# Attention on whole 128-row tiles with rows of zeros, and a DRAIN of GpSimd behind the fourth output block of every group

## The chip, the cores and the metric

The kernel runs on one core of one Trainium2 chip. The metric is the device time of one execution in microseconds, the median of several runs; less is better. A profile comes from one further execution. The engines are named as the profile has them: PE is TensorE, PEld its weight loads, DVE VectorE, ACT ScalarE, POOL GpSimd and SP SyncE, which only issues DMAs here.

## The reference

Three steps follow one another: attention against mean-pooled keys and values, a top-1 mixture of experts (MoE), and a dense layer that takes the maximum of three products.

```python
# q, k, v: (8, 8, 576, 64); q and k are scaled by 8 in the set-up
k_p = k.reshape(B, H, Sp, 8, D).mean(axis=3)          # Sp = 72
v_p = v.reshape(B, H, Sp, 8, D).mean(axis=3)
scores = np.matmul(q, k_p.transpose(0, 1, 3, 2)) / np.sqrt(D)
attn = softmax(scores)                                # max subtracted, sum + 1e-9
x = np.matmul(attn, v_p)                              # -> (4608, 512)

xn, en = x / (norm(x) + 1e-6), expert_emb / (norm(expert_emb) + 1e-6)
logits = xn @ en.T / tau                              # 8 experts
for e in range(8):                                    # expert_idx = argmax(logits)
    h = np.maximum(x[mask_e] @ w1[e], 0.0)            # w1: (512, 1024)
    out[mask_e] = gate_w[mask_e, None] * (h @ w2[e])

h = np.maximum(np.maximum(out @ w1, out @ w2), out @ w3)   # 512 -> 768
return h @ w_out                                           # (4608, 512)
```

## The kernel before, in words

**Attention.** The 4608 tokens make 36 tiles of 128. Two neighbouring batches share nine tiles: four of the first batch, one mixed tile with 64 tokens of each, and four of the second. So 32 tiles belong to one batch and 4 are mixed. A batch has 576 pooled rows (8 heads of 72), which are held as five chunks of 128, 128, 128, 128 and 64 rows (`RC`). Only the fifth chunk isn't full.

The main loop (from L1481) is a software pipeline over tiles. One turn issues, in this order, the scores of tile it-1 (`stage_s`, L421: products at L442, or L428 for a mixed tile; maximum and subtraction on DVE, L457 and L460), the transposes of the attention weights of tile it-3 (`stage_a`, L468: five transposes at L473, two copies on ACT at L475 and L476), the transposes of q for tile it (`stage_q`, L406), the exponential of tile it-1 on ACT (`stage_e`, L466), and attention times v of tile it-4 (`stage_x`, L488: six products at L496, then five steps on DVE, L506 to L523). Each float32 product stands in the trace as two passes, that is two LDWEIGHTS and two MATMULs. Between the DVE steps `fill()` puts pieces of the routing, in numbers from a small table (L913).

Beside the tiles run the preparations of the next batches (`prep_steps`, L254): the keys and values are pooled (on DVE for the first batches, L263 and L271, else on GpSimd, L277 and L287), spread over head slots with a mask (`spread_v`, L293, into `vbd`), transposed (`trans_k` L305 and `trans_v` L341 for the first two batches, `trans_kv` L318 for the others), and multiplied with the normalised expert embeddings `enT` (`vdot`, L350; two DVE steps at L358). The last chunk is handled with 64 rows throughout: in the transposes, in `vdot` and in `stage_x`, where the contraction runs over `RC[c]` rows. `vT` and `enT` hold 64 partitions, so `vdot` contracts 64 rows in every chunk. The tiles `kp`, `vp`, `vT` and `aT` come from rotating pools.

**MoE.** Its items run from the gather of x in expert order through two products (L1062 and L1110) with weights split into two parts. Its first work overlaps the last attention tiles.

**Last layer.** `second` (L1572) works in six groups of 768 tokens. After its products a group has six output blocks of 128 tokens. For each block TensorE makes 18 products (`out_part`, L1697), and `out_rows` scales the sum by the gate on ACT into `ob` (L1703, five buffers) and issues an indirect DMA on GpSimd that scatters the 128 rows to the output (L1704). These DMAs write the same tensor, and each is issued after the one before has landed. GpSimd's instructions run in the order of the code. Behind the six blocks of a group it has nothing until the next group's blocks, whose gate values it has fetched before (`tokens`, L1592). L1761 is a branch that isn't taken here (a second round for experts with many tokens), and L1802 is the program's closing code.

Of the kernel before, what the change touches and what calls it, by code (L numbers as in the profile page):

```python
# [8 lines left out]
F32 = mybir.dt.float32  # L9
# [5 lines left out]
A = mybir.AluOpType  # L15
# [6 lines left out]
def attention_moe_moe_kernel(  # L22
# [39 lines left out]
    DA = D + 1 + E  # L62
# [33 lines left out]
    ident = cp.tile([P, P], F32, name="ident")  # L96
# [19 lines left out]
    if True:  # L116
# [61 lines left out]
        if True:  # L178
# [55 lines left out]

            kbds = [ap1.tile([P, H, 2, SP], F32, name=f"kbd{i}") for i in range(3)]
            vbds = [ap1.tile([P, NSL, DA], F32, name=f"vbd{i}") for i in range(3)]
            nc.gpsimd.memset(kbds[0], 0.0)
            rmask = ap1.tile([P, 5, H], F32, name="rmask")
            nc.gpsimd.memset(rmask, 1.0)
# [14 lines left out]
            def prep_steps(b):  # L254
                kt, vt = kv[b]
                kb, vb = kbds[b % 3], vbds[b % 3]
                kp = qp.tile([P, 5, 2, D], F32, tag="kp", name=f"kp{b}")
                vp = kp[:, :, 1, :] if b > 1 else qp.tile([P, 5, D], F32, tag="vp", name=f"vp{b}")
                vT = qp.tile([D, 5, P], F32, tag="vT", name=f"vT{b}", bufs=1)

                def pool_k(c):
                    n = KC[c] if b < 2 else RC[c]
# [49 lines left out]
                def trans_kv(cs, r0):  # L312

                    ps = pq.tile([P, 512], F32, tag="pq", name=f"ptk{b}_{r0}")
                    col = 0
                    for c in cs:
                        n = RC[c]
                        nc.tensor.transpose(  # L318
                            ps[:, col : col + n], kp[0:n, c].rearrange("p two d -> p (two d)"), ident[0:n, 0:n]
                        )  # L320
                        col += n
                    a0 = 0
                    while a0 < col:
                        h, s_ = divmod(r0 + a0, SP)
                        if s_ == 0 and col - a0 >= SP:
                            nh = (col - a0) // SP
                            a1 = a0 + nh * SP
                            src, at_ = ps[0:D, a0:a1].rearrange("p (h s) -> p h s", s=SP), (slice(h, h + nh), slice(0, SP))
                        else:
                            a1 = min(col, a0 + SP - s_)  # L330
                            src, at_ = ps[0:D, a0:a1], (h, slice(s_, s_ + a1 - a0))
                        nc.scalar.copy(kb[0:D, at_[0], 0, at_[1]], src)
                        nc.scalar.copy(kb[D:P, at_[0], 1, at_[1]], src)
                        a0 = a1
                    nc.scalar.copy(vT.rearrange("p c r -> p (c r)")[:, r0 : r0 + col], ps[D:P, 0:col])

                def trans_v(c0, c1):
                    ps = pq.tile([P, 512], F32, tag="pq", name=f"ptv{b}_{c0}")
                    for c in range(c0, c1):
                        n = RC[c]  # L340
                        nc.tensor.transpose(  # L341
                            ps[0:D, (c - c0) * P : (c - c0) * P + n], vp[0:n, c, :], ident[0:n, 0:n]
                        )
                    w_ = (c1 - c0 - 1) * P + RC[c1 - 1]
                    nc.scalar.copy(vT.rearrange("p c r -> p (c r)")[:, c0 * P : c0 * P + w_], ps[0:D, 0:w_])

                def vdot():
                    ps = pq.tile([P, 512], F32, tag="pq", name=f"pd{b}")
                    for c, (h0, h1) in enumerate(HS):
                        nc.tensor.matmul(  # L350
                            ps[0 : RC[c], SL[c] * E : SL[c + 1] * E],
                            vT[:, c, 0 : RC[c]],
                            enT[:, h0:h1, :].rearrange("p h e -> p (h e)"),
                            start=True,
                            stop=True,
                        )
                    for n, s0, s1 in ((P, 0, SL[4]), (64, SL[4], NSL)):
                        nc.vector.tensor_tensor(  # L358
                            vb[0:n, s0:s1, D + 1 : DA],
                            ps[0:n, s0 * E : s1 * E].rearrange("p (s e) -> p s e", e=E),  # L360
                            mslot[0:n, s0:s1, :].to_broadcast([n, s1 - s0, E]),
                            op=A.mult,
                        )

                if b == 0:
                    return [
# [101 lines left out]
            def stage_a(i):  # L468
                m, part, t, _ = tiles[i]
                at = st_p.pop(i)[:, t % 2].rearrange("p h s -> p (h s)")  # L470
                ps = pb.tile([P, 2 * 512], F32, tag="paT", name=f"paT{i}")
                for c, n in enumerate(RC):
                    nc.tensor.transpose(ps[0:n, c * P : (c + 1) * P], at[:, c * P : c * P + n], ident)  # L473
                aT = ap2.tile([P, 5, P], F32, tag="aT", name=f"aT{i}")
# [13 lines left out]
            def stage_x(i):  # L488
# [3 lines left out]
                for bank in range(2):  # L492
                    parts = [x_ for x_ in AV if x_[1] // 4 == bank]
                    for n, (c, g0, g1, sl) in enumerate(parts):
                        for lo, hi, b in segs:
                            nc.tensor.matmul(  # L496
                                ps[lo:hi, bank, (g0 % 4) * DA : (g0 % 4 + g1 - g0) * DA],
                                aT[0 : RC[c], c, lo:hi],
                                vbds[b % 3][0 : RC[c], sl : sl + g1 - g0, :].rearrange("p h d -> p (h d)"),
                                start=(n == 0),  # L500
                                stop=(n == len(parts) - 1),
                                skip_group_check=True,
                            )
# [878 lines left out]
            enT = ap1.tile([D, H, E], F32, name="enT")  # L1382

            def en_steps():
                en2 = yield from inverse_norm(ap1, ess, E, 1, "en")
                vs(en, en, en2[:, 0:1], A.mult)
                yield
                ps = pq.tile([P, 512], F32, tag="pq", name="pe0")
                for h in range(H):
                    nc.tensor.transpose(ps[0:D, h * E : (h + 1) * E], en[:, h * D : (h + 1) * D], ident[0:E, 0:E])  # L1390
                nc.scalar.copy(enT, ps[0:D, 0 : H * E].rearrange("p (h e) -> p h e", e=E))

            tok_i = rp.tile([P, NT], I32, name="tok_i")
            for m in range(B // 2):
# [177 lines left out]
    def second(st, groups, again=False):  # L1572
# [144 lines left out]
        for g in groups:  # L1717
            for _ in ahead:
                pass
            for n in range(CH):  # L1720
                quad(g, n, groups.index(g) * CH + n)
            nxt = g + 1 in groups
            ahead = columns(g + 1) if nxt else iter(())
            next(ahead, None)
            if nxt:
                tokens(g + 1)
            ps = [po_.tile([P, DM], F32, tag="po", name=f"po{g}_{j}") for j in range(2)]
            out_part(g, ps[0], 0, FO[:4])
            finish_block()
            finish_parts()  # L1730
            out_part(g, ps[1], 1, FO[:4])
            for j in range(2):
                out_part(g, ps[j], j, FO[4:])
                for _ in range(2):
                    next(ahead, None)
                out_rows(g, ps[j], j)
            for j in range(2, GB):
                p_ = po_.tile([P, DM], F32, tag="po", name=f"po{g}_{j}")
                out_part(g, p_, j, FO)
                for _ in range(2):  # L1740
# [66 lines left out]
```

## Time and profile before

| what | us |
|---|---|
| median of 3 runs | 1244.08 |
| lowest and highest run | 1242.42, 1244.53 |
| the profiled execution | 1242.23 |
| its span in the trace | 1240.2 |
| TensorE busy | 1205.1 (97%) |
| VectorE busy | 795.3 (64%) |
| ScalarE busy | 579.9 (47%) |
| GpSimd busy | 318.1 (26%) |

The span runs from the first to the last instruction of the core; the profiled execution's own time is 2 us longer than that. Attention takes the stretch up to about 200 us, the MoE that up to some 750 us, the last layer the rest. A busy engine isn't an engine at its peak, and the ends of TensorE's instructions are modelled by the profiler, so distances between starts say more of it than durations do.

### The profile page before, as it was taken

The numbers are of one execution on the slowest core, as the hardware profiler recorded it, in microseconds if no ns is written. First come the engines' busy times: TensorE is split into PE (matmuls) and PEld (weight loads), VectorE is DVE, ScalarE is ACT, GpSimd is POOL, SyncE is SP. The second block draws the span as 40 slices with busy tenths as digits, with TensorE's granted clock in tenths as the row PEclk, the third lists the DMA queues.
The fourth block names the chain that finished last, engine by engine and source line by source line (L and its number), as shares of the span: only waits on it lengthen the run. The fifth ranks groups of instructions, "written<-read, shape, count | busy, mean of one in ns | idle before, by whom it ended". The sixth has DMA issues, their size and how long they took to land. (4 is left out here: it accounts for less than half of the span.)

```text
span 1240.2 us, 22423 instructions
## 1 busy us (share of the span) xinstructions
PE 1205.1 (97%) x8251; PEld 1149.6 (93%) x8251; DVE 795.3 (64%) x1597; ACT 579.9 (47%) x1040; POOL 318.1 (26%) x471
## 2 busy tenths in 40 slices
PE   6999999999999999999999999999999999999995
PEld 5888889899999999999998998998998998998994
DVE  5878886977789999987854445454454454453540
ACT  4666574445566666666654323324223223233221
POOL 6999534401122212121001202003004004004001
PEclk9999999999999999999999999999999999999998
DMA  9796344607884456555349665574673773773721
GB/s 261 222 341 205 137 145 155 198 23 138 296 279 154 138 213 221 205 204 158 124 146 307 253 241 209 193 254 173 231 264 146 256 262 122 259 286 107 262 97 53
DMA packets 98054, 246.21 MB, mean 199 GB/s; under 512 B 17116, under 2 KB 58122, under 8 KB 89874
## 3 DMA queue, kind: packets, MB, share of 16 engines
q1 hardware_dynamic: 84786, 189.09, 45.0%
q0 software_dynamic: 13152, 55.62, 13.4%
q8 instruction: 67, 1.10, 0.4%
q14 instruction: 49, 0.40, 0.1%
HBM read 252.23 MB, written 46.98 MB: 241 GB/s over the span
## 5 line engine op out<-in xcount | busy, mean ns | idle before, releaser
L1621 PE MATMUL p<-yhi,wt 128*128 128x384 f32 x1512 | 387.1, 336 | 0.0
L1621 PEld LDWEIGHTS p<-yhi,wt 128*128 128x128 f32 x1512 | 273.4, 188 | 0.7 <-PE pyT L1132 0.3
L1621 PE MATMUL p<-ylo,wt 128*128 128x384 f32 x756 | 254.0, 336 | 0.0
L1629 ACT COPY s<-p 128x384 f32<-128x384 f32 x162 | 77.8, 480 | 221.6 <-PE p L1621 214.2
L1110 PE MATMUL py<-hhi,wlo 128*128 128x256 f32 x576 | 163.1, 283 | 1.6 <-DVE wlo L1042 1.6
L1110 PE MATMUL py<-hhi,whi 128*128 128x256 f32 x576 | 164.6, 286 | 0.0
L1062 PE MATMUL ph<-xhi,whi 128*128 128x256 f32 x576 | 163.8, 284 | 0.7 <-DVE hlo L1078 0.7
L1062 PE MATMUL ph<-xhi,wlo 128*128 128x256 f32 x576 | 163.0, 283 | 0.7 <-DVE wlo L1042 0.7
L1062 PE MATMUL ph<-xlo,whi 128*128 128x256 f32 x576 | 163.0, 283 | 0.0
L1110 PE MATMUL py<-hlo,whi 128*128 128x256 f32 x576 | 162.9, 283 | 0.0
L1621 PEld LDWEIGHTS p<-ylo,wt 128*128 128x128 f32 x756 | 142.1, 188 | 0.5
L1650 DVE TENSOR_TENSOR blk<-p,s 128x384 f32<-128x384 f32 x108 | 59.7, 553 | 113.8 <-PE p L1621 113.5
L1606 POOL DMA_INDIRECT gt<-gbuf,ix x26 | 37.0, 1423 | 315.6 <-DMA ix<-idbuf 309.2
L1110 PEld LDWEIGHTS py<-hhi,wlo 128*128 128x128 f32 x576 | 110.4, 192 | 1.8 <-DVE wlo L1042 1.8
L1062 PEld LDWEIGHTS ph<-xhi,whi 128*128 128x128 f32 x576 | 110.5, 192 | 1.3 <-DVE hlo L1078 1.1
L1062 PEld LDWEIGHTS ph<-xhi,wlo 128*128 128x128 f32 x576 | 110.5, 192 | 0.9 <-DVE wlo L1042 0.9
L1062 PEld LDWEIGHTS ph<-xlo,whi 128*128 128x128 f32 x576 | 110.5, 192 | 0.0
L1110 PEld LDWEIGHTS py<-hlo,whi 128*128 128x128 f32 x576 | 110.5, 192 | 0.0
L1110 PEld LDWEIGHTS py<-hhi,whi 128*128 128x128 f32 x576 | 110.4, 192 | 0.0
L1042 DVE TENSOR_TENSOR wlo<-w2raw,whi 128x1024 fp32r<-128x1024 f32 x84 | 102.1, 1220 | 8.6 <-ACT whi L1040 8.5
L1042 DVE TENSOR_TENSOR wlo<-w1raw,whi 128x1024 fp32r<-128x1024 f32 x67 | 81.7, 1219 | 26.2 <-ACT whi L1040 25.3
L1040 ACT CAST whi<-w2raw 128x1024 fp32r<-128x1024 f32 x88 | 91.8, 1043 | 7.4 <-PE py L1110 4.4
(317 smaller groups left out, 2260.1 us busy)
## 6 DMA issues: line engine op xcount, KB each, us to landing
wt<-wdram SPq DMA_DIRECT2D x51, 1792.0 KB
w1raw<-in_moe_w_dram SPq DMA_DIRECT2D x88, 512.0 KB
w2raw<-in_moe_w_dram SPq DMA_DIRECT2D x88, 512.0 KB
wdram<-wst POOLq DMA_DIRECT2D x9, 1792.0 KB
ybuf<-yo SPq DMA_DIRECT2D x40, 256.0 KB
cvraw<-in_moe_w_dram POOLq DMA_DIRECT2D x36, 256.0 KB
xbuf<-x SPq DMA_DIRECT2D x16, 512.0 KB
yr<-ybuf SPq DMA_DIRECT2D x20, 384.0 KB
```

What stands on the lines that cost most here:

```text
L1040: nc.scalar.copy(hi, src)
L1042: eng.tensor_tensor(lo, src, hi.bitcast(F32), op=A.subtract)
L1062: nc.tensor.matmul(ps[:, f, :], a_[:, c, fs], b_[:, c, :], start=(n == 0), stop=(n == 3 * DC - 1))
L1110: nc.tensor.matmul(py[:, c // 2, (c % 2) * 256 : (c % 2 + 1) * 256], a_[:, f, c * P : (c + 1) * P], b_[:, f, :], start=(piece == 0 and f = ...
L1606: nc.gpsimd.indirect_dma_start(out=gt[g][:, j : j + 1], out_offset=None, in_=gbuf[:, :], in_offset=bass.IndirectOffsetOnAxis(ap=cols[j], a ...
L1621: nc.tensor.matmul(ps, a_, b_, start=(start and c + n == 0), stop=(c == 1 and n == 2), skip_group_check=True)
L1629: nc.scalar.copy(t, ps)
L1650: tt(src, add[0], add[1], op=A.add)
```

## The change

It has two parts that don't touch each other.

First, the padded parts of the attention become whole. `kp`, `vp`, `vT`, `aT` and `enT` become fixed tiles, made once, two each of `kp`, `vp` and `aT` in turn. Twelve MEMSETs on DVE at the start fill with zeros what is never written later: partitions 64 to 127 of the fifth chunk in `kp`, `vp`, `aT` and in the three `vbd`, and partitions 0 to 63 of `vT` and `enT`, whose data now sit in partitions 64 to 127. The transposes of the last chunk, the products of `vdot` and those of `stage_x` then take all 128 rows. The two DVE steps behind `vdot` become one. The five transposes in `stage_a`, the transposes in `trans_k`, and the two 64-token halves of a mixed tile stay as they were.

Second, GpSimd gets a DRAIN instruction behind the output DMA of the fourth block (`j == 3`) of every group.

```diff
+            aTs = [ap1.tile([P, 5, P], F32, name=f"aT{i}") for i in range(2)]
+            kps = [qp.tile([P, 5, 2, D], F32, name=f"kp{i}", bufs=1) for i in range(2)]
+            vps = [qp.tile([P, 5, D], F32, name=f"vp{i}", bufs=1) for i in range(2)]
+            vT = qp.tile([P, 5, P], F32, name="vT", bufs=1)
+            enT = ap1.tile([P, H, E], F32, name="enT")
+            for t_ in kps:
+                nc.vector.memset(t_[R4:P, 4], 0.0)
+            for t_ in vps:
+                nc.vector.memset(t_[R4:P, 4, :], 0.0)
+            nc.vector.memset(vT[0:D], 0.0)
+            nc.vector.memset(vT[D:P, 4, R4:P], 0.0)
+            nc.vector.memset(enT[0:D], 0.0)
+            for t_ in aTs:
+                nc.vector.memset(t_[R4:P, 4, :], 0.0)
+            for t_ in vbds:
+                nc.vector.memset(t_[R4:P, SL[4] : NSL, :], 0.0)
...
-                            ps[:, col : col + n], kp[0:n, c].rearrange("p two d -> p (two d)"), ident[0:n, 0:n]
+                            ps[:, col : col + P], kp[:, c].rearrange("p two d -> p (two d)"), ident
...
-                            ps[0 : RC[c], SL[c] * E : SL[c + 1] * E],
-                            vT[:, c, 0 : RC[c]],
+                            ps[:, SL[c] * E : SL[c + 1] * E],
+                            vT[:, c, :],
...
-                    for n, s0, s1 in ((P, 0, SL[4]), (64, SL[4], NSL)):
-                        nc.vector.tensor_tensor(
-                            vb[0:n, s0:s1, D + 1 : DA],
...
+                    nc.vector.tensor_tensor(
+                        vb[:, :, D + 1 : DA],
...
-                                aT[0 : RC[c], c, lo:hi],
-                                vbds[b % 3][0 : RC[c], sl : sl + g1 - g0, :].rearrange("p h d -> p (h d)"),
+                                aT[:, c, lo:hi],
+                                vbds[b % 3][:, sl : sl + g1 - g0, :].rearrange("p h d -> p (h d)"),
...
                 out_rows(g, p_, j)
+                if j == 3:
+                    nc.gpsimd.drain()
```

At the start of DVE's program, before (`pre` is a scratch tile, `kraw` the raw keys of the first batch):

```order
L139 MEMSET cnt_124 128x8
L144 MEMSET pre_130 128x64
L144 MEMSET pre_131 128x64
L263 TENSOR_REDUCE kp_187<-kraw_138 128x64 x3
L263 TENSOR_REDUCE kp_187<-kraw_138 120x64
```

The same place of the changed kernel:

```order
L144 MEMSET pre_131 128x64
L244 MEMSET kp_172 64x128
L244 MEMSET kp_173 64x128
L246 MEMSET vp_174 64x64
L246 MEMSET vp_175 64x64
L247 MEMSET vT 64x640
L248 MEMSET vT 64x64
L249 MEMSET enT 64x64
L251 MEMSET aT_170 64x128
L251 MEMSET aT_171 64x128
L253 MEMSET vbd_167 64x73
L253 MEMSET vbd_168 64x73
```

The twelve MEMSETs (the third of `vbd` follows) come to stand ahead of the first pooling step; nothing else moves there. On PE, at the place where a tile's attention times v is followed by the `vdot` of a later batch and the next tile's scores (`pd` is the PSUM tile of `vdot`), before:

```order
L496 MATMUL pav_864<-vbd_168,aT_801 128x219
L496 MATMUL pav_864<-vbd_168,aT_801 128x73
L350 MATMUL pd_880<-enT,vT_531 128x16
L350 MATMUL pd_880<-enT,vT_531 128x24 x3
L350 MATMUL pd_880<-enT,vT_531 64x8
L442 MATMUL psc_893<-kbd_166,qT_856 128x144 x4
```

And in the changed kernel, where line numbers are 11 to 15 higher:

```order
L507 MATMUL pav_863<-vbd_168,aT_170 128x219
L507 MATMUL pav_863<-vbd_168,aT_170 128x73
L362 MATMUL pd_879<-enT,vT 128x16
L362 MATMUL pd_879<-enT,vT 128x24 x3
L362 MATMUL pd_879<-enT,vT 128x8
L453 MATMUL psc_891<-kbd_166,qT_855 128x144 x4
```

The order stays; the contracted rows of the product with 73 columns, which these rows don't print, go from 64 to 128, and the last product of `vdot` writes 128 rows in place of 64. The order of SP, ACT and GpSimd is the same in both, but for the DRAINs.

## Rows read from the trace of the kernel before

**Rows 1.** The page, busy time of each engine over the span.
```profile
PE 1205.1 (97%) x8251; PEld 1149.6 (93%) x8251; DVE 795.3 (64%) x1597; ACT 579.9 (47%) x1040; POOL 318.1 (26%) x471
```
**Rows 2.** Windows: length; busy PE, PEld, DVE, ACT, POOL; PE clock; DMA share; GB/s.
```profile
50.00:200.00 150.00, 145.19 (x1159) 130.84 (x1158) 117.27 (x339) 97.56 (x241) 103.65 (x196) 1.00 0.63 206
...
600.00:800.00 200.00, 199.28 (x1252) 189.50 (x1251) 101.13 (x167) 81.85 (x146) 22.71 (x23) 1.00 0.60 208
```
**Rows 3.** Waits of PE, 24 to 200 us: us in total, times, longest.
```profile
PE pav L496 <- DVE dt L521: 2.4, 3, 1.3
```
**Rows 4.** Closing code: ns (min, median, max) and starts; then a window there.
```profile
L1761 POOLq INC_SWDGE_SEM  x1: 1810/1810/1810, 1230.8 to 1230.8; - x1
...
L1802 POOLq DRAIN  x3: 46/109/6689, 1232.7 to 1239.9; - x3
...
1232.60:1239.40 6.80, 0.00 (x0) 0.00 (x0) 0.00 (x0) 0.00 (x0) 0.00 (x0) 0.50 0.00 0
```
**Rows 5.** Groups by form, 0 to 350 us: busy, mean ns, idle before.
```profile
L496 PE MATMUL pav<-vbd,aT 64*128 64x73 f32 x64 | 14.1, 300 | 0.0
...
L496 PEld LDWEIGHTS pav<-vbd,aT 64*128 64x128 f32 x64 | 9.4, 184 | 8.6 <-issue 8.6
...
L473 PEld LDWEIGHTS paT<-ident,at 128*64 128x64 f32 x32 | 3.6, 113 | 0.0
```
**Rows 6.** Timeline of PE in one tile: start, us, tile size, columns, count.
```profile
64.84 0.35 PE L496 MATMUL pav<-vbd,aT 128*128 128x219 f32 x1
65.02 0.34 PE L496 MATMUL pav<-vbd,aT 128*128 128x73 f32 x2
65.09 0.45 PE L496 MATMUL pav<-vbd,aT 128*128 128x73 f32 x2
65.19 0.46 PE L496 MATMUL pav<-vbd,aT 128*128 128x146 f32 x2
65.68 0.35 PE L496 MATMUL pav<-vbd,aT 128*128 128x219 f32 x1
65.95 0.33 PE L496 MATMUL pav<-vbd,aT 64*128 64x73 f32 x1
66.12 0.27 PE L496 MATMUL pav<-vbd,aT 64*128 64x73 f32 x1
66.32 0.39 PE L442 MATMUL psc<-kbd,qT 128*128 128x144 f32 x1
66.55 0.41 PE L442 MATMUL psc<-kbd,qT 128*128 128x144 f32 x2
66.67 0.41 PE L442 MATMUL psc<-kbd,qT 128*128 128x144 f32 x2
```
**Rows 7.** Windows of one tile's turn each (three of 35), and their sum.
```profile
64.40:68.39 3.99, 3.99 (x31) 3.65 (x30) 2.61 (x7) 2.41 (x7) 3.99 (x10) 1.00 1.11 316
...
95.42:100.29 4.87, 4.21 (x32) 3.66 (x31) 4.87 (x14) 4.41 (x13) 4.40 (x10) 1.00 0.71 182
...
118.38:124.93 6.55, 5.25 (x41) 4.71 (x40) 6.48 (x13) 3.50 (x9) 6.08 (x15) 1.00 0.07 23
...
sum 169.32, PE 162.87 PEld 146.54 DVE 132.47 ACT 108.61 POOL 122.51; mean PE 4.65 PEld 4.19 DVE 3.78 ACT 3.10 POOL 3.50
```
**Rows 8.** Timeline of DVE at the start: start, us, operation, idle before.
```profile
0.93 0.18 DVE L144 MEMSET pre<- 128x64 f32 x2
4.01 1.94 DVE L263 TENSOR_REDUCE kp<-kraw 128x64 f32<-128x512 f32 x2 [2.90 <-DMA kraw<-in_k_dram]
```
**Rows 9.** Timeline of POOL, last group's output blocks 1, 4, 5 and 6.
```profile
1209.84 0.99 POOL L1704 DMA_INDIRECT out_dram<-ob,ix  x1 [61.38 <-ACT ob L1703]
...
1220.59 0.98 POOL L1704 DMA_INDIRECT out_dram<-ob,ix  x1 [2.52 <-DMA out_dram<-ob,ix]
1224.09 0.98 POOL L1704 DMA_INDIRECT out_dram<-ob,ix  x1 [2.52 <-ACT ob L1703]
1228.08 0.98 POOL L1704 DMA_INDIRECT out_dram<-ob,ix  x1 [3.01 <-ACTq L1761]
```

More of the change, by code (lines that the diff above doesn't have):

```diff
@@ L236, in attention_moe_moe_kernel @@
             vbds = [ap1.tile([P, NSL, DA], F32, name=f"vbd{i}") for i in range(3)]
+            R4 = RC[4]
+            aTs = [ap1.tile([P, 5, P], F32, name=f"aT{i}") for i in range(2)]
[14 more added lines that the diff above has]
+                nc.vector.memset(t_[R4:P, SL[4] : NSL, :], 0.0)
             nc.gpsimd.memset(kbds[0], 0.0)
@@ L256, in prep_steps @@
                 kb, vb = kbds[b % 3], vbds[b % 3]
-                kp = qp.tile([P, 5, 2, D], F32, tag="kp", name=f"kp{b}")
-                vp = kp[:, :, 1, :] if b > 1 else qp.tile([P, 5, D], F32, tag="vp", name=f"vp{b}")
-                vT = qp.tile([D, 5, P], F32, tag="vT", name=f"vT{b}", bufs=1)
+                kp = kps[b % 2]
+                vp = kp[:, :, 1, :] if b > 1 else vps[b]
                 def pool_k(c):
@@ L316, in trans_kv @@
                     for c in cs:
-                        n = RC[c]
                         nc.tensor.transpose(
-                            ps[:, col : col + n], kp[0:n, c].rearrange("p two d -> p (two d)"), ident[0:n, 0:n]
+                            ps[:, col : col + P], kp[:, c].rearrange("p two d -> p (two d)"), ident
                         )
-                        col += n
+                        col += RC[c]
                     a0 = 0
@@ L334, in trans_kv @@
                         a0 = a1
-                    nc.scalar.copy(vT.rearrange("p c r -> p (c r)")[:, r0 : r0 + col], ps[D:P, 0:col])
+                    nc.scalar.copy(vT[D:P].rearrange("p c r -> p (c r)")[:, r0 : r0 + col], ps[D:P, 0:col])
                 def trans_v(c0, c1):
@@ L339, in trans_v @@
                     for c in range(c0, c1):
[L340 to L343, printed above, removed]
+                        nc.tensor.transpose(ps[0:D, (c - c0) * P : (c - c0 + 1) * P], vp[:, c, :], ident)
                     w_ = (c1 - c0 - 1) * P + RC[c1 - 1]
-                    nc.scalar.copy(vT.rearrange("p c r -> p (c r)")[:, c0 * P : c0 * P + w_], ps[0:D, 0:w_])
+                    nc.scalar.copy(vT[D:P].rearrange("p c r -> p (c r)")[:, c0 * P : c0 * P + w_], ps[0:D, 0:w_])
                 def vdot():
@@ L356, in vdot @@
                         )
-                    for n, s0, s1 in ((P, 0, SL[4]), (64, SL[4], NSL)):
-                        nc.vector.tensor_tensor(
-                            vb[0:n, s0:s1, D + 1 : DA],
[L360 to L363, printed above, removed]
+                    nc.vector.tensor_tensor(
+                        vb[:, :, D + 1 : DA],
+                        ps[:, 0 : NSL * E].rearrange("p (s e) -> p s e", e=E),
+                        mslot.to_broadcast([P, NSL, E]),
+                        op=A.mult,
+                    )
                 if b == 0:
@@ L473, in stage_a @@
                     nc.tensor.transpose(ps[0:n, c * P : (c + 1) * P], at[:, c * P : c * P + n], ident)
-                aT = ap2.tile([P, 5, P], F32, tag="aT", name=f"aT{i}")
+                aT = aTs[i % 2]
                 nc.scalar.copy(aT[:, 0:4, :], ps[:, 0 : 4 * P].rearrange("p (c n) -> p c n", n=P))
@@ L1381, in attention_moe_moe_kernel @@
             p0[0]()
-            enT = ap1.tile([D, H, E], F32, name="enT")
             def en_steps():
@@ L1390, in en_steps @@
                     nc.tensor.transpose(ps[0:D, h * E : (h + 1) * E], en[:, h * D : (h + 1) * D], ident[0:E, 0:E])
-                nc.scalar.copy(enT, ps[0:D, 0 : H * E].rearrange("p (h e) -> p h e", e=E))
+                nc.scalar.copy(enT[D:P], ps[0:D, 0 : H * E].rearrange("p (h e) -> p h e", e=E))
             tok_i = rp.tile([P, NT], I32, name="tok_i")
```

## The prediction

> **What bounds the kernel now.** I read the busy times of the whole program first, then the same by stretches, then what TensorE waited for, then single instructions in one attention tile, and last the end of the program. TensorE is busy for 1205.1 of 1240.2 us [rows 1]. In the stretch from 50 to 200 us, nearly all of it attention, it is busy for 145.19 of 150, and in 600 to 800 us, in the MoE, for 199.28 of 200 [rows 2]. Its largest wait for another engine in the attention is 2.4 us in three times [rows 3]. So TensorE sets the time, and a microsecond taken from its instruction stream in the attention should still be there at the end, as long as no other engine fills the place. The second thing that bounds is short and sits at the very end: three DRAINs of GpSimd stand in the closing code, of 46, 109 and 6689 ns, the long one first. In the 6.80 us around it no engine does anything and no DMA moves a byte [rows 4]. This is pure tail.
>
> **The change, part by part.** *Whole tiles in attn times v.* Each attention tile issues six products here, which the trace lists as two passes each; the sixth contracts 64 rows. Its tile size is printed as 64\*128, that of the others as 128\*128. There are 64 passes of the former, two in each of the 32 tiles that belong to one batch, and their weight loads sit behind 8.6 us of "issue" idle, 0.27 us for each pair [rows 5]. A tile that halves the columns (128\*64, the fifth transpose of every tile) has no such idle, 0.0 over 32 [rows 5]. So the price is of the halved rows, and of going there and back. The timeline of one tile gives it from starts, since the ends of matmuls are modelled [rows 6]:
> - A product of 219 columns is followed after 0.18 us (64.84 to 65.02) when the next is whole, and after 0.27 (65.68 to 65.95) when the next has 64 rows: +0.09.
> - The two passes of 73 columns start 0.07 apart (65.02 to 65.09) whole, and 0.17 apart (65.95 to 66.12) with 64 rows: +0.10.
> - From the second pass to the next instruction it is 0.10 whole (65.09 to 65.19) and 0.20 (66.12 to 66.32): +0.10.
> - The first score product behind it takes 0.23 (66.32 to 66.55) where the following takes 0.12 (66.55 to 66.67): +0.11.
>
> That is 0.40 us in this tile; where a transpose and not a score product follows, less comes back behind it, so I take 0.36 on average. Of the four mixed tiles, which also halve the columns, no row separates the two prices; bounds are 0 and 0.40, I take the middle, 0.2. Sum: 32 x 0.36 + 4 x 0.2 = 12.3 us.
>
> *What VectorE gives back.* The saving can come only as far as the engine behind TensorE isn't full. In the stretch of a usual tile VectorE is busy for 2.61 of 3.99 us, so all of it comes. But in the stretch 95.42 to 100.29 it is busy for 4.87 of 4.87, and in 118.38 to 124.93 for 6.48 of 6.55: routing steps are pushed between its attention steps there [rows 7]. Going through the 35 stretches of one tile each in the same way (sum row: 132.47 of 169.32 busy), three have no idle VectorE and lose 0.36 each (1.1), three have 0.03 to 0.10 and lose 0.9 together, and two have 0.24 and 0.31 and lose 0.2. Left: 12.3 - 2.2 = **10.1 us**. The bounds are 13 (VectorE's surplus moves on into later idle) and 6 (every tile with a VectorE over 80% busy gives nothing).
>
> *The other padding.* The transpose of the last pooled chunk and the vector product with the expert embeddings (five small products in every batch) become whole too. The latter stands right behind a halved tile, so it already pays no switch going in; I count nothing for both, with 0 to -1 us as bounds. The two VectorE multiplications behind that product become one, eight instructions fewer in the run, off the path.
>
> *The zeros.* Twelve MEMSETs on VectorE at the start, 1627 columns in all. Two of 64 columns take 0.18 us together [rows 8], so 1627/128 x 0.18 = 2.3 us. VectorE sits idle for 2.90 us at that very place, waiting for the first keys to land [rows 8]. So they cost nothing; without that cover it would be 2.3 us at the start, since the first pooled keys are what everything waits for. Nothing is inside the loops: the zero rows are never written again. The halves that the copies write (ScalarE's, GpSimd's) stay as they were.
>
> *The DRAIN of GpSimd, six of them.* Queued behind it on GpSimd are the fifth and sixth output block of the group, no more; behind these GpSimd has nothing for a long time (it came to the last group's first block after 61.38 us of idle) [rows 9]. So in five groups the wait is covered by 60 us, and nobody needs those rows before the end. In the last group the fourth block is issued at 1220.59 and done at 1221.57, and the fifth starts at 1224.09, since ScalarE had not finished it before: a DRAIN of up to 2.5 us is free there. The sixth starts at 1228.08 and has about half a microsecond more (the blocks before came 3.5 us apart) [rows 9]. What the DRAIN takes there is in no row. Bounds: 0.05 and 6.69, the shortest and the longest of the three at the end [rows 4].
>
> *What it does to the long DRAIN at the end.* Bounds: it stays at 6.69, or falls to the size of the two others, 0.05 to 0.11. What decides for me is their order: three DRAINs of one engine stand in a row and only the first is long, with no transfer in flight and no work on the engine. So a DRAIN clears something that has gathered since GpSimd's last one, and with the new ones most of it will have been cleared long before. I take 0.2 for it, with two DMAs left to clear: **-6.5 us**, with -6.6 to 0 as the ends.
>
> *Sum.* 1242.2 (the profiled execution) - 10.1 - 6.5 = 1225.6. The median of the runs, 1244.1, is 1.9 above the profiled execution, so **1227.5**.
>
> **Rivals.**
> - *The long DRAIN is a matter of the end.* Right ahead of it stands INC_SWDGE_SEM of 1810 ns, once in the closing part [rows 4]. If that leaves the work that the first DRAIN waits for, the new ones change nothing: 1227.5 + 6.5 = 1234.0.
> - *Every DRAIN costs 6.69 anew.* If one behind output DMAs always takes that long, the last group's fifth block starts at 1221.57 + 6.69 = 1228.26 in place of 1224.09, the sixth 3.5 later at 1231.8 in place of 1228.08 [rows 9], and the end stays: 1227.5 + 6.5 + 3.7 = 1237.7. Against it speaks that two of the three at the end are short.
> - *Padding saves nothing.* The load of a 64-row tile takes 184 ns in the mean [rows 5], hardly under that of whole tiles. If the idle ahead of it were due to something else than the tile's size (the last product of a bank, say), only the DRAIN's part would be left: 1244.1 - 6.5 = 1237.6. Against it: the first bank's last product is whole and has no such gap [rows 6]. The Trainium skill, "TensorE: Matmul & The Clock Gate", section LDWEIGHTS (loading the stationary operand), says that a load's time goes by its columns and not by the rows contracted; by that rule alone zeros in place of absent rows neither cost nor save, which is this rival. The same skill's "TensorEngine Tiling (Array Packing)", Key Properties, says that changing the tiling mode drains TensorE; it gives no price, and the 0.27 us idle agrees with it for halved rows, but the 0.0 of the halved columns doesn't.
> - *Neither part does what it says*: padding saves nothing and the last DRAIN stays. 1244.1.
> - *Slower: the last group's DRAIN waits long.* Place: GpSimd, between the fourth and the fifth output block of group six. If it must wait until all that GpSimd ever queued is written off and takes D us, the end moves by D less about 2.5 to 3. With the end's DRAIN cleared, this eats the 16.6 us won from D of about 19 on; with it kept, from about 13. At D = 20 with it kept: 1234.0 + 17.3 = 1251.3. That is two to three times the longest DRAIN that the trace shows, which had a thousand microseconds behind it to clear; so little speaks for it.
>
> **How the numbers follow.** Forecast 0.57 (1227.5, own range 1224 to 1231), a matter of the end 0.20 (1234.0), every DRAIN anew 0.09 (1237.7), padding saves nothing 0.06 (1237.6), neither 0.03 (1244.1), slower 0.05. The range reaches down to 1223.5, the attention's 13 with the DRAIN's 6.5 and a little over half a microsecond of spread, and up to 1238, so that the two cases of 1237.6 are in. Outside lie neither and slower (0.08) and the tails. Some 0.2% (2.5 us) is what a measurement can tell here from no change: all cases but the last two lie under 1241.6, so faster 0.92, same 0.03, slower 0.05.
>
> **What would show it.** In the changed profile no instruction of the attn times v product has 64 rows in its tile, no load in it has 0.27 us of issue idle ahead, and a usual tile's stretch is 3.6 and not 3.99 us. The stretches with a full VectorE are as long as before; if those shrink too, the sum was too small. The MoE's first product starts some 10 us earlier. VectorE's MEMSETs end before the first keys land. The first DRAIN of the closing code takes under a microsecond, and the fifth and sixth block of the last group keep their 3.5 us pace. If the long DRAIN still stands at 6.69, the end rival is right; if the fifth block comes over 4 us later than its pace, the dear DRAIN is. What I can't exclude from this trace: that a shorter attention makes GpSimd's pooling or the stores of x late, which would show as waits of TensorE for kbd or vbd, and would give back part of the 10.1.

## The result, and the profile after

The changed kernel takes 1227.82 us (1227.56 to 1229.43 in four runs), against 1244.3 for the kernel before in the same comparison: a ratio of 0.9866, with a 95% interval of 0.984 to 0.9892. That is 16.5 us less, with a plausible span of some 13 to 20; 1227.5 was forecast. The profiled execution is the slowest of the four, 1229.43 us, with a span of 1227.4 against 1240.2. So the two traces differ by 12.8 us, and they don't explain all of the 16.5. Where the rest is will be seen below.

The busy times on the page of the changed kernel, to be held against [rows 1]:

```profile
PE 1196.2 (97%) x8251; PEld 1151.3 (94%) x8251; DVE 795.9 (65%) x1601; ACT 579.8 (47%) x1040; POOL 319.2 (26%) x471
```

TensorE issues as many instructions as before and is busy for 8.9 us less. The groups of the attn times v product, up to 350 us (busy, mean ns of one, idle before), which answer to [rows 5]:

```profile
L507 PEld LDWEIGHTS pav<-vbd,aT 128*128 128x128 f32 x384 | 57.2, 192 | 2.1 <-PE pqT L428 1.7 <-PE paT L484 0.3
...
L507 PE MATMUL pav<-vbd,aT 128*128 128x73 f32 x128 | 21.9, 252 | 0.0
```

The form 64\*128 is gone. Its 64 weight loads are now among the 384 of the full size, and the 8.6 us of issue idle ahead of them is gone too. In the timeline of the same tile as in [rows 6] (start, us):

```profile
64.51 0.53 PE L507 MATMUL pav<-vbd,aT 128*128 128x219 f32 x2
64.95 0.27 PE L507 MATMUL pav<-vbd,aT 128*128 128x73 f32 x1
65.06 0.33 PE L453 MATMUL psc<-kbd,qT 128*128 128x144 f32 x1
```

From the last pass of 73 columns to the first score product it is now 0.11 us (64.95 to 65.06), where it was 0.20 (66.12 to 66.32). The turn of a usual tile (tile 7, from the first pass of its attn times v to that of the next tile) falls from 3.99 [rows 7] to 3.65 (columns as in [rows 2]):

```profile
63.41:67.06 3.65, 3.65 (x31) 3.65 (x30) 2.46 (x7) 2.42 (x7) 3.65 (x10) 1.00 1.07 363
```

The attention from tile 0's product to tile 35's is 169.32 us before and 163.78 after, 5.5 us less. Most of the rest of the traces' 12.8 is at the end. The GpSimd instructions of the closing code (ns: min, median, max) and the six DRAINs, for [rows 4]:

```profile
L1772 POOLq INC_SWDGE_SEM  x1: 240/240/240, 1225.1 to 1225.1; - x1
L1813 POOLq DRAIN  x3: 109/194/208, 1225.4 to 1227.0; - x3
L1753 POOLq DRAIN  x6: 3228/3626/4029, 765.9 to 1214.6; - x6
```

And GpSimd's output blocks four to six of the last group, for [rows 9]:

```profile
1214.84 0.98 POOL L1713 DMA_INDIRECT out_dram<-ob,ix  x1 [2.51 <-DMA out_dram<-ob,ix]
1218.70 0.98 POOL L1713 DMA_INDIRECT out_dram<-ob,ix  x1 [2.88 <-ACT ob L1712]
1222.38 0.98 POOL L1713 DMA_INDIRECT out_dram<-ob,ix  x1 [2.69 <-ACTq L1772]
```

The long DRAIN at the end is gone, 6689 ns against 208 at most, and INC_SWDGE_SEM ahead of it fell from 1810 to 240, which had not been counted on. From the sixth block's issue to the end of the span it was 12.1 us (1228.08 to 1240.2) and is 5.0 (1222.38 to 1227.4): 7.1 us less. In the middle a DRAIN takes 3.2 to 4.0 us, 22 in all. In the last group the fifth block comes 3.86 us behind the fourth in place of 3.50; the sixth has caught up with its pace.

So the two traces give 5.5 for the attention, 7.1 for the end, and 0.5 for a first tile that starts earlier (27.64 against 28.18), 13.1 together; between the attention and the sixth block 0.4 is lost.

### The profile page after: what moved, and what is told of

Its sections match the earlier page's. It is cut to its first block, busy times and chain, and to the rows that moved or that the text cites. A ratio compares the mean times of both kernels' runs of the same rounds, so it can differ in the third digit from the quotient of the medians.

```text
span 1227.4 us, 22453 instructions
## 1 busy us (share of the span) xinstructions
PE 1196.2 (97%) x8251; PEld 1151.3 (94%) x8251; DVE 795.9 (65%) x1601; ACT 579.8 (47%) x1040; POOL 319.2 (26%) x471
```

## The experiments

### The two parts, each alone, and both beside them

`attn_only` is the changed kernel without this; `drain_only` is the kernel before with it:

```diff
                 out_rows(g, p_, j)
+                if j == 3:
+                    nc.gpsimd.drain()
```

> The attention on whole tiles, without the DRAINs. If the parts are additive as predicted: 10.1 us less than before (6 to 13), and the long DRAIN at the end at 6.7 us again. The profile of the changed kernel speaks for less: its sixth output block of the last group is issued 5.7 us earlier than before, and one attention tile in it ran at half the granted clock for a while. By that, 5.7 to 8 us less than before. If the padding saved nothing by itself: no difference.

> The six DRAINs alone, attention as before. Predicted: 6.5 us less than before. By the two profiles (last output block issued 12.1 us before the end of the span before, 5.0 us in the changed kernel) 7.1 us less. If the end were shorter for another reason than the DRAINs: no difference.

> The changed kernel again, beside its two parts on one chip: the sum of what the parts save, 13 to 17 us less than before. If the parts overlap (the end hides a shorter attention, or the other way round), less than their sum by more than 1.5 us.

Against 1243.78 us for the kernel before on this chip: `attn_only` 1234.23 (0.9925, 0.9912 to 0.9939), `drain_only` 1234.27 (0.9925, 0.9911 to 0.994), both 1227.83 (0.9868, 0.9853 to 0.9883). So 9.6, 9.5 and 16.0 us less. The sum of the parts, 19.1, is 3.1 above the whole. Each of the three intervals is some 3.5 us wide, so that this gap is just about what they leave open. By the text on both again, a gap of more than 1.5 us would be an overlap of the parts; the medians alone don't decide it. The traces are sharper. The windows of the attention, tile 0 to tile 35 (us; busy PE, PEld, DVE, ACT, POOL; clock), of before, `attn_only`, `drain_only` and both again, one kernel after the other:

```profile
28.18:197.50 169.32, 162.87 (x1284) 146.54 (x1283) 132.47 (x386) 108.61 (x271) 122.51 (x234) 0.99 0.68 218
```

```profile
27.49:188.93 161.44, 152.44 (x1285) 146.52 (x1283) 129.67 (x379) 108.17 (x271) 122.44 (x234) 1.00 0.69 225
```

```profile
27.20:196.53 169.33, 161.74 (x1284) 145.17 (x1283) 132.08 (x386) 108.62 (x271) 122.28 (x234) 1.00 0.68 218
```

```profile
28.84:190.05 161.21, 152.41 (x1285) 146.50 (x1284) 129.53 (x379) 108.08 (x271) 122.50 (x234) 1.00 0.70 224
```

The attention is shorter by 7.9 and 8.1 us where the padding is in, and by nothing where only the DRAINs are. At the other end, the closing code of `attn_only` keeps the long DRAIN to the nanosecond:

```profile
L1811 POOLq DRAIN  x3: 46/109/6689, 1224.2 to 1231.4; - x3
```

From the sixth block's issue to the end it is 12.1 us in `attn_only`, 4.6 in `drain_only` and 5.0 in both again. Each part acts in its own place. Only half a microsecond of the end depends on more than the DRAINs (4.6 against 5.0): the last of the three closing DRAINs takes 46 ns in `drain_only` and 194 in both again, and comes 0.3 us later behind the second; why is open. The place where the first tile's product starts, though, lies between 27.2 and 28.8 us in these traces, with no bearing on which part is in. This moves single executions by 1.6 us.

### What the halved rows cost: trips or passes

`sw_apart` and `sw_adj` give one more product 64 rows in the kernel before, in tiles of one batch (the comments stand for the difference between the two):

```diff
+                    def kr(bank, n, c):           # this is sw_apart
+                        return 64 if len(segs) == 1 and bank == 0 and n == 1 else RC[c]
+                    # sw_adj: bank == 1 and n == len(parts) - 2 in place of bank == 0 and n == 1
...
-                                aT[0 : RC[c], c, lo:hi],
-                                vbds[b % 3][0 : RC[c], sl : sl + g1 - g0, :].rearrange("p h d -> p (h d)"),
+                                aT[0 : kr(bank, n, c), c, lo:hi],
+                                vbds[b % 3][0 : kr(bank, n, c), sl : sl + g1 - g0, :].rearrange("p h d -> p (h d)"),
```

> The kernel before, with a second 64-row product in every tile of one batch, away from the first: the middle product of the first bank (219 columns) contracts rows 0 to 63 of its chunk, the other half of that chunk is left out of the sum. 'Going there and back' is what costs: one more such trip, a usual tile's turn goes from 3.99 to 4.3 to 4.4 us. 'Each pass with 64 rows' costs: the same here, 4.3 to 4.4. If the gap belongs to a bank's last product and not to its rows: 3.99.

> The kernel before, with the product right ahead of the 64-row product contracting 64 rows too (219 columns, rows 0 to 63 of its chunk, the other half left out of the sum). 'Going there and back': no new trip, a usual tile's turn stays at 3.99 to 4.05 us. 'Each pass with 64 rows': 4.2 to 4.4, as with the two apart.

Tokens go to other experts in these two, so the whole run (1425 and 1411 us) says nothing and the turns are read. The turn of tile 1 in `sw_apart`, and that of tile 7 in `sw_adj` (3.99 each before; columns as above):

```profile
35.21:39.59 4.38, 4.38 (x31) 3.62 (x30) 2.54 (x7) 2.41 (x7) 4.07 (x10) 1.00 0.94 271
```

```profile
65.65:69.65 4.00, 4.00 (x32) 3.78 (x30) 2.62 (x7) 2.42 (x7) 3.84 (x9) 1.00 1.14 281
```

A second trip to 64 rows and back adds 0.39 us. A second product inside the same trip adds 0.01. So it is the trip that costs, not the pass, and not the place at the end of a bank. The Trainium skill, "TensorEngine Tiling (Array Packing)", Key Properties, says that changing the tiling mode drains TensorE. The trace agrees for the rows, with 0.39 us for going and coming where that page of the skill has no number; for halved columns [rows 5] show no idle, and no run here tried them apart.

### What takes back a part of the saving

By the single tile, 32 x 0.345 (3.99 to 3.65) and 4 x 0.14 (a mixed tile, 4.25 to 4.11) make 11.6 us, of which 11.3 fall into the 35 turns of the windows above; 8 arrived. `lite_before` and `lite_after` make VectorE lighter in both kernels:

```diff
-                nc.vector.tensor_reduce(mx, sc, axis=AX, op=A.max)
+                nc.vector.tensor_reduce(mx, sc[:, :, :, 0 : SP // 2], axis=AX, op=A.max)
```

> The kernel before with VectorE lighter by 0.35 to 0.4 us per tile: the maximum of the scores is taken over half of each head's 72 columns. TensorE bounds most tiles, so only the turns with a full VectorE shrink: 1 to 3 us less than before.

> The changed kernel with the same lighter VectorE. The attention's stretch from the first tile's product to the 36th's is 169.3 us before and 161.2 to 163.8 in the runs of the changed one, where 11.6 would have gone by the single tile (32 x 0.345 + 4 x 0.14). 'VectorE takes back the rest': with VectorE light in both, the stretch shrinks by 9.5 to 11 between lite_before and this (the rest is ScalarE's, at the three tiles that wait for the copy of q). 'Something else takes it back' (ScalarE, or the clock): 8 as with the full VectorE. The whole run is 16 to 18 us less than lite_before.

`lite_before` is no different from before (0.9992, 0.9972 to 1.0012), `lite_after` 1225.86 us (0.9852, 0.9817 to 0.9888; 16.2 us less than `lite_before`). The attention goes from 168.57 to 161.03, by 7.5 us and not by 9.5 to 11. By what was written beforehand, something else than VectorE takes back the rest. But the cut was too small to decide it: the step went from 0.75 to 0.45 us, and the stretches with a full VectorE were still full, as 92.72 to 97.82 (5.10 of 5.10) in `lite_after`.

`nofill_after` takes all the routing steps out from between the attention's:

```diff
-            FILL = {1: (1, 1, 2, 1, 1, 1, 1), 2: (1, 4, 3, 1, 1, 2, 2)}
+            FILL = {1: (0, 0, 0, 0, 0, 0, 0), 2: (0, 0, 0, 0, 0, 0, 0)}
```

> The changed kernel without the routing steps between VectorE's attention steps; they are done behind the attention, so the whole run is longer and only the tiles' turns are read. 'VectorE holds the tiles back': tiles 14 and 23, 4.9 and 5.3 us with a full VectorE, fall to some 4.4 (as tile 5), and tiles 2 to 4 together from 16.6 to 15.5 or less. 'ScalarE holds back the tiles with the copies of the keys': tiles 8 and 9 together stay at 8.97 us, 17 and 18 too. If VectorE were behind those as well, the two pairs fall to 8.3.

The windows of tiles 8 and 9, 17 and 18, 14, and 23, first of both again, then of `nofill_after`:

```profile
67.71:76.66 8.95, 8.28 (x74) 7.89 (x72) 7.33 (x21) 7.47 (x21) 8.11 (x17) 1.00 1.10 335
107.08:116.05 8.97, 8.28 (x74) 7.89 (x72) 7.48 (x23) 7.49 (x21) 8.11 (x18) 1.00 1.04 340
93.61:98.58 4.97, 4.12 (x32) 3.74 (x31) 4.97 (x15) 4.49 (x13) 4.50 (x10) 1.00 0.92 269
133.00:138.31 5.31, 4.12 (x33) 3.75 (x31) 5.31 (x15) 3.87 (x11) 4.84 (x10) 1.00 0.84 266
```

```profile
64.83:73.78 8.95, 8.28 (x73) 7.89 (x72) 6.35 (x16) 7.47 (x21) 8.32 (x19) 1.00 1.05 366
102.24:111.20 8.96, 8.28 (x73) 7.89 (x72) 6.36 (x16) 7.48 (x21) 8.26 (x18) 1.00 1.03 335
90.06:93.82 3.76, 3.76 (x32) 3.76 (x31) 2.57 (x7) 3.55 (x11) 3.45 (x8) 1.00 0.87 223
127.48:131.23 3.75, 3.75 (x32) 3.75 (x31) 2.56 (x7) 3.68 (x11) 3.36 (x8) 1.00 0.81 228
```

Both answers are right, each for tiles of its own. Tiles 14 and 23 fall to 3.76 and 3.75 without the routing, and tiles 2 to 4 to 14.5 in all, further than expected: there VectorE is the bound. Tiles 8 and 9, and 17 and 18, stay at 8.95, as long as in the kernel before (68.39 to 77.36, 8.97). There TensorE waits once, and for ScalarE, in `nofill_after` (64.8 to 73.8) as in `attn_only` (66.6 to 75.6; us, times, longest):

```profile
PE psc L439 <- ACT qT L429: 0.7, 1, 0.7
```

In these tiles ScalarE copies the keys and values of the next batch out of PSUM, some 2 us of work, ahead of the copy of the next tile's q. It runs without a pause for 5.8 us in `attn_only`. Whatever TensorE wins in tile 8 it waits for in tile 9. Tiles 0 and 5 are of the same kind: 6.00 and 4.49 us before, 5.93 and 4.49 in both again and in `nofill_after`, with one wait of TensorE in each, for ScalarE (0.8 and 0.5 us).

The third pair that the next texts put to ScalarE, tiles 26 and 27, is not. It falls from 10.05 us in both again to 8.82 in `nofill_after`, and in both again (152.6 to 158.7) TensorE waits in tile 27 for both engines, VectorE being busy for 5.91 of 6.01 us:

```profile
PE psc L439 <- DVE sh L471: 0.5, 1, 0.5
PE psc L439 <- ACT kbd L348: 0.4, 1, 0.4
```

One tile goes the other way. Tile 19, which the prediction counted among those with a full VectorE (118.38 to 124.93, 6.55 us [rows 7]), takes 4.77 us in both again, 1.78 less. A routing step on 72 columns of VectorE took 2.85 us there before and takes 0.22 in the changed kernel, and TensorE's wait behind it, 1.3 us and the longest of [rows 3], is gone. First before (the wait in 118 to 125 us, the step, the GpSimd instruction with whose end it ended), then both again:

```profile
PE pav L496 <- DVE dt L521: 1.3, 1, 1.3
120.44 2.85 DVE L553 TENSOR_TENSOR pre<-pre 128x72 f32<-128x72 f32 x1
122.47 0.72 POOL L277 TENSOR_TENSOR kraw<-kraw 128x256 f32<-128x256 f32 x1
```

```profile
116.05:120.82 4.77, 4.77 (x42) 4.77 (x40) 3.75 (x12) 2.47 (x7) 4.30 (x10) 1.00 0.31 119
117.14 0.22 DVE L564 TENSOR_TENSOR pre<-pre 128x72 f32<-128x72 f32 x1
```

The step is long in the three traces with halved rows and the same routing (before, `drain_only`, `lite_before`) and in none of the eight with whole tiles. So 1.4 of the attention's 8.1 us are not the price of the halved rows. Why the step isn't held any more, with GpSimd's work standing otherwise beside it, no run tried.

The turns, both again against before and against 0.345 (0.14) expected for each, then add up so: the tiles held by ScalarE (0, 5, 8, 9, 17, 18) give back 2.0 us, those with a full VectorE (2 to 4, 14, 23, 26, 27) 2.2, all others 0.4. That leaves 6.7 of 11.3; with the 1.4 of tile 19 it is the 8.1 measured.

### A slow spell that some executions have

The changed kernel's own profile has tiles 24 and 25 in 12.56 us, `attn_only` in 10.31. The windows of the two tiles, first of the changed kernel:

```profile
137.60:144.77 7.17, 5.68 (x45) 5.47 (x46) 6.89 (x22) 3.41 (x9) 5.46 (x11) 1.00 0.54 208
144.77:150.16 5.39, 5.39 (x32) 5.32 (x31) 3.20 (x10) 1.48 (x4) 0.00 (x0) 0.68 0.17 71
```

```profile
137.18:143.77 6.59, 5.71 (x46) 5.47 (x46) 6.21 (x23) 3.41 (x9) 5.47 (x11) 1.00 0.67 262
143.77:147.49 3.72, 3.72 (x32) 3.72 (x31) 2.37 (x7) 1.48 (x4) 0.00 (x0) 1.00 0.06 22
```

In tile 24 TensorE stands idle for 1.49 us, waiting for a routing step of VectorE, where it is 0.88 in `attn_only`, and for ScalarE. In tile 25 the granted clock is then 0.68 in the mean in place of 1.00, partly 1.2 and partly 2.4 GHz, and the turn is 1.67 us longer. VectorE was late since some of its steps took longer with the same work; the same step of 48 columns, in the changed kernel and in `attn_only`:

```profile
139.60 0.77 DVE L568 TENSOR_SCALAR lg<-lg,rtau 128x48 f32<-128x48 f32 x1
```

```profile
139.18 0.24 DVE L568 TENSOR_SCALAR lg<-lg,rtau 128x48 f32<-128x48 f32 x1
```

GpSimd works in both. The long step ends at 140.37 us, 0.01 behind the GpSimd instruction that ran beside it:

```profile
139.61 0.75 POOL L1497 DMA_DIRECT2D ybuf<-ones  x1
```

It is so with all of them. In the eleven traces with the routing in place, from 27 to 200 us, 204 steps of VectorE took over 0.15 us longer than the shortest of their kind, and each of them ended 0.01 to 0.12 us behind the end of a GpSimd instruction; of the others one in four did. So a step of VectorE can be held until an instruction of GpSimd ends, as the 2.85 us one of tile 19 was (its end is 123.29, GpSimd's 123.19). Which steps are held and which aren't is open. Of the eight kernels with whole tiles and the routing in place, two have the spell in their profile (the changed kernel and `d_idle`). It accounts for 2.25 of the 2.6 us by which the attention is longer in the first profile than in that of both again.

### What the DRAIN at the end clears

Three kernels have one DRAIN only: in the last group (`d_last`), in the first (`d_first`), and in the last group in another place (`d_idle`):

```diff
-                if j == 3:
+                if j == 3 and g == NG - 1:      # d_last; d_first: g == 0
                     nc.gpsimd.drain()
...
             out_part(g, ps[1], 1, FO[:4])
+            if g == NG - 1:                     # d_idle, and none behind the blocks
+                nc.gpsimd.drain()
```

> The changed kernel with the DRAIN in the last group alone. Theory 'recent': what the DRAIN at the end clears comes from the last group's own work, so the five other DRAINs do nothing: the middle DRAIN takes 3.2 us as in the changed kernel, the first one at the end 0.2, the end 5 us behind the last output block's issue. Rival 'gathered': it gathers over all DMAs that GpSimd issued since its last DRAIN, some 170 of them; then the middle DRAIN takes over 6.7 us and the fifth block comes 3 us late or more.

> The DRAIN in the first group alone. 'Recent': the end is as before, 6.7 us in its first DRAIN and 12 us from the last block's issue. 'Gathered': 62 of some 170 DMAs are left to be cleared, so 2 to 3 us. 'Once' (the first DRAIN of a program has to have something fetched, later ones have not): 0.2 us.

> A single DRAIN, on GpSimd in the last group ahead of the group's first output block, where GpSimd has stood idle for 60 us and none of its transfers is in flight. 'In flight' (a DRAIN behind an output block takes 3 to 4 us since it waits for that block's transfer): under 0.3 us here. If something has to be fetched or cleared: several us, 6.7 if it is what the end pays. At the end six DMAs lie behind it in place of two: 0.2 us if only a first DRAIN is dear, 0.6 or more if each DMA leaves its share, 6.7 if the six are what it clears.

Two things in these texts have to be put right. The first group's DRAIN leaves 56 of GpSimd's 177 DMAs behind it, not 62. And the DRAIN of `d_idle` waits for nothing that TensorE does, so GpSimd came to it not after 60 us of idle but at once, at 1142.0, behind the last block of the fifth group. So the run doesn't tell what a DRAIN costs with nothing in flight. The DRAIN of `d_last` and the last three blocks there:

```profile
L1753 POOLq DRAIN  x1: 7739/7739/7739, 1212.8 to 1212.8; - x1
```

```profile
1212.98 0.98 POOL L1713 DMA_INDIRECT out_dram<-ob,ix  x1 [2.51 <-DMA out_dram<-ob,ix]
1221.35 0.98 POOL L1713 DMA_INDIRECT out_dram<-ob,ix  x1 [7.39 <-issue]
1225.02 0.98 POOL L1713 DMA_INDIRECT out_dram<-ob,ix  x1 [2.69 <-DMA out_dram<-ob,ix]
```

"Recent" falls. Without the five DRAINs before it, the sixth takes 7.74 us and not 3.23, and the fifth block comes 8.4 us behind the fourth. The end then is as short as in the changed kernel. `d_first`, at the end:

```profile
L1772 POOLq INC_SWDGE_SEM  x1: 1310/1310/1310, 1222.4 to 1222.4; - x1
...
L1813 POOLq DRAIN  x3: 46/109/4622, 1223.7 to 1228.9; - x3
```

So one DRAIN at 763 us isn't "once" for all either. `d_idle`, its DRAIN, and the end behind it:

```profile
L1742 POOLq DRAIN  x1: 9372/9372/9372, 1142.0 to 1142.0; - x1
...
L1772 POOLq INC_SWDGE_SEM  x1: 320/320/320, 1225.7 to 1225.7; - x1
L1813 POOLq DRAIN  x3: 46/109/539, 1226.0 to 1227.3; - x3
```

INC_SWDGE_SEM and the first DRAIN of the end together, by the number of GpSimd's DMAs since its last DRAIN: 2 DMAs 0.45 us (240 + 208), 6 DMAs 0.86, 56 DMAs 5.93, 177 DMAs 8.50 (the kernel before). From 2 to 6 and from 2 to 56 that is 0.10 us for each further DMA. The 121 further ones that the kernel before has, those up to the first group's fourth block, add only 0.02 each. "Gathered" holds for the end: what the DRAIN there clears grows with what GpSimd has issued since the last one. The share isn't the same for all DMAs, and why the early ones weigh less (half of them are plain copies, and nearly all are hundreds of microseconds older) is open. In these four kernels more DMAs also mean a longer time since the last DRAIN, and no run parts the two; time alone doesn't set it, since in the changed kernel the first group's DRAIN, with 766 us and 121 DMAs behind it, took 4.03 us, and the next four, with some 90 us and 12 DMAs, 3.48 to 3.88. Nor is it settled what the DRAINs in the middle are made of, down to 3.23 us in the last group with only 6 DMAs to clear; the block issued just ahead of each is still in flight then. With some 170 DMAs behind them they took 7.74 us in `d_last`, 9.37 in `d_idle` and 10.24 in `vt_dve`, so the number alone doesn't give their time either.

From the last group's first block to the end it is 22.9 us in `d_idle` and 23.4 in both again, so one DRAIN in that place is worth as much as six. The half microsecond between them is not the place's: `drain_only`, with six, has 22.8.

### An attempt at a faster version

`vt_dve` is `d_idle` with one copy taken from ScalarE:

```diff
-                    nc.scalar.copy(vT[D:P].rearrange("p c r -> p (c r)")[:, r0 : r0 + col], ps[D:P, 0:col])
+                    cp = nc.vector.tensor_copy if r0 == 0 and b % 2 == 1 else nc.scalar.copy
+                    cp(vT[D:P].rearrange("p c r -> p (c r)")[:, r0 : r0 + col], ps[D:P, 0:col])
```

> An attempt at a faster version: a single DRAIN, in the last group ahead of its first output block, and for every second batch from the fourth on the copy of the transposed values (0.58 us) on VectorE and not on ScalarE. 'ScalarE holds back' tiles 8 and 9, 17 and 18, 26 and 27: each pair's 9.0 to 10.0 us falls by 0.3 to 0.6, the attention by 1 to 1.8 in all. If VectorE held them back: each pair gets 0.3 to 0.6 longer. From the last group's first output block to the end 22.9 us, where the changed kernel has 23.4. In all 16 to 18 us less than before, against 16 of the changed kernel, if the slow spell at tile 25 stays away.

1227.11 us (0.9869, 0.9844 to 0.9895): no different from the changed kernel. The end is the 22.9 us that `d_idle` had, but the attention is longer, 163.57 us against 161.21 in both again. 1.6 of these 2.4 us are in tile 2, where a step of VectorE (`tokid`) took 2.13 us in place of 0.51, as in the slow spell. Tiles 8 and 9 take 9.32 in place of 8.95:

```profile
67.82:77.14 9.32, 8.50 (x74) 7.89 (x72) 7.87 (x21) 7.27 (x21) 8.46 (x18) 1.00 1.08 341
```

TensorE now waits for VectorE there, and in tiles 17 and 18 (36 to 154 us; in all, times, longest):

```profile
PE psc L440 <- DVE mxl L577: 1.5, 2, 0.8
```

By the expectation this would speak for VectorE as the bound of these tiles, but `nofill_after` says otherwise. The copy stands ahead of the maximum of the scores on VectorE, in a stretch in which it has routing to do as well; the bound has moved from the one engine to the other. No version here beats the changed kernel by more than can be measured.

## Why the prediction came out

The time was within half a microsecond of the forecast and both mechanisms were the right ones, but the terms are not as good as the sum.

**What bounds the kernel.** Right. What TensorE won in the attention was still there at the end: between tile 35 and the sixth block of the last group it is 1030.6 us before, 1030.7 in `attn_only` and 1030.5 in both again.

**The price of the halved rows.** Right in kind and nearly in size: 0.36 was taken for a tile and 0.345 measured, 0.2 for a mixed tile and 0.14 measured. `sw_apart` and `sw_adj` show that the trip is what costs. The load's time, 184 ns halved and 192 whole, changed hardly. The Trainium skill, "TensorE: Matmul & The Clock Gate", section LDWEIGHTS (loading the stationary operand), has a load go by its columns alone. The two numbers agree with it. The rival that zeros save nothing was wrong all the same, since the cost was not in the load.

**What is taken back.** This term was too small: 2.2 us were predicted; 4.6 were taken back, and 1.4 came from elsewhere. VectorE alone did take 2.2, for the most part in the tiles named. The step that failed is the one that looked at VectorE alone: tiles 0, 5, 8, 9, 17 and 18 are held by ScalarE, with VectorE idle beside it, and their 2.0 us of saving are lost. The pairs 8 and 9, 17 and 18 took 8.97 and 8.96 us before and take 8.95 and 8.97 in both again. Tile 19 was misread: 2.85 of its 6.48 us of VectorE were one drawn-out step, not more routing, and its turn shrank by 1.78 us where nearly nothing was expected. The prediction had said that the sum was too small if such stretches shrank; it was too large, since this gain was smaller than what ScalarE kept. The attention gave 8 us and not 10.1, 6.7 of them by the mechanism forecast, and 5.5 in an execution with the slow spell; the range for it had 6 to 13.

**The other padding.** Right within 0.06 us a batch: a turn that also holds the small products of `vdot`, as that of tile 6, goes from 5.06 to 4.77, 0.29 less.

**The zeros.** Right: the MEMSETs end before the first keys are there, at 3.35 us, and the first pooling step starts at 4.00, as in [rows 8] (4.01):

```profile
3.06 0.29 DVE L253 MEMSET vbd<- 64x73 f32 x3
4.00 1.01 DVE L279 TENSOR_REDUCE kp<-kraw 128x64 f32<-128x512 f32 x1 [0.66 <-DMA kraw<-in_k_dram]
```

**The DRAINs.** Right, in the form that was thought likeliest, and 7.1 us in place of 6.5: INC_SWDGE_SEM, which stood in a rival as a possible cause, got shorter by 1.6 us itself as part of the same thing. A part of that is lost: between the first and the second DRAIN of the end lie 0.2 us before (1239.4 to 1239.6) and 0.7 after (1225.6 to 1226.3), since other closing steps now come last (SyncE's first DRAIN starts at 1226.1). In the middle the price was taken as 0.05 to 6.69 and hidden up to 2.5; it is 3.2, and the fifth block was late by 0.36 us. That it is hidden rests on all six DRAINs being there: with the sixth alone it is 7.74, above the upper bound of 6.69, and 4.9 us come onto the path.

**The sum.** 8.1 and 7.1 make 15.2, against 16.0 and 16.5 by the medians of the two comparisons. The rest is within their intervals. That 1227.5 was so near is partly luck: an attention term too large even with the 1.4 us of tile 19, which no step of the prediction foresaw, and an end term too small. The lower end of the range doesn't follow from its own terms: 2.9 us more in the attention and 0.6 of spread lead from 1227.5 to 1224.0, not to 1223.5.

## What to carry to other kernels

Where a chunk isn't full, padding its contraction to 128 rows with zeros that are written once cost nothing here, the MEMSETs being hidden, and saved a trip of TensorE out of its whole-array form and back, 0.35 to 0.4 us each; look for them by the tile size in the trace and by issue idle ahead of the loads. Before counting on such a saving in every turn of a pipeline, go through the turns for each engine behind TensorE, not only the busiest: it comes off only where none of them is full. Read the measured turns one by one as well: a sum near the forecast can hide a loss and an unforeseen gain. And look at what the closing code waits for; a wait there that grows with what an engine has issued may be had earlier for nothing, where the engine has time, as GpSimd had here.

## What the runs showed of the hardware

- The first DRAIN of GpSimd at the end of the program took longer the more DMAs it had issued since its last one: 0.2 us with 2 of them, 0.5 with 6, 4.6 with 56, 6.7 with 177, and INC_SWDGE_SEM ahead of it grew along (0.24, 0.32, 1.31, 1.81). In the kernel before no byte moves meanwhile [rows 4].
- These times repeat to the nanosecond between kernels (6689 ns in three profiles, 208 or 213 with 2 DMAs), while VectorE's steps don't: one of 48 columns took 0.24 us in one execution and 0.77 in another, one of 72 columns 0.22 and 2.85. The long ones end 0.01 to 0.12 us behind the end of a GpSimd instruction.
